# Output rows in two pieces of six products, read by ScalarE and summed by GpSimd, in a two-branch attention kernel

## The chip, the cores and the metric

The kernel runs on one core of a Trainium2 chip. The metric is the device time of one execution in microseconds (us). A core has a matrix engine (TensorE, PE in the profile; its weight loads are PEld), a vector engine (VectorE, DVE), a scalar engine (ScalarE, ACT), a general engine (GpSimd, POOL) and a queue that issues DMAs (SyncE, SP). Each engine works through its own list of instructions in order, and they wait for each other by semaphores. TensorE writes its results to PSUM, eight banks of 128 x 512 float32; the other tiles lie in SBUF.

## The reference, cut to what matters

The input x is 2048 x 512. Two attention branches with 32 heads of 16 columns share it, and a gate mixes them.

```
g = sigmoid(sum(x * gate_w))                      # one number a row
a = A(x): 4 segments of 512 rows; in each, causal softmax attention within the segment,
    plus a memory term phi(q) M / phi(q) z from the segments before; mixed by sigmoid(beta); @ wo
b = B(x): softmax attention over all 2048 rows; @ wo_b
out = g * a + (1 - g) * b
```

The part that the change touches works on the scaled attention outputs o of both branches: out = o_A @ wo + o_B @ wo_b, 128 rows at a time.

## The kernel before

**Units, slots, groups.** Queries are cut into four chunks of 512 rows, heads into eight quads. One (chunk, quad) is a unit: 32 of branch A (u = 0 to 31) and 32 of branch B (u = 32 to 63). The main loop has 32 slots; slot k computes unit 32 + k of B and then unit k of A. A slot has 37 groups n: 0 to 31 for the 16 key blocks of B (two heads each), 32 to 36 for the four key blocks of A. All instructions are written out in this order (`manual_schedule`), so the code's order is the order in each engine's list.

**What a group does.** `t_group` multiplies K with Q for two heads (L635) into two banks out of three (tb0, tb1, mb, the least lately used first; in slot 31 five, with two of the score banks), and ScalarE takes the exponential (L641) into one of two tile sets `raw`. Between the two products, in most groups, stands a score product for the next unit (`s_b`, L572, two matmuls into one of two buffers `sbk`), of which VectorE takes the row maxima (L574); in groups 32 to 36 these are scores of A (L550, L554, maxima L558, L560). Then `pvs` adds a V product (`pv`, L657): exponentials times V for four heads, into the one bank `pvb`. Key block `it` of B is multiplied in groups 2 it + 2 and 2 it + 3, 256 of the 512 queries in each. For A, GpSimd first sets the masked entries of the diagonal blocks to zero (L644). A's products are 0 in groups 34 and 35 by halves, 1 and 3 in group 36, and 2 in group 0 of the next slot.

**What follows a unit.** `fin_copy` copies `pvb` to a tile `pvs`: for B in group 33 and for A in group 0 of the next slot; `pvb` may be written again only then. By way of DRAM its sums come back as `rec`, VectorE takes the reciprocals (L681, groups 11 and 13), GpSimd scales them and, every second slot, normalises a whole output tile (`fin_norm`, L701, L706; it waits for the DMA that brings the factors `d`). `m_chain` (after group 21) and `m_rows` (group 24) turn the maxima into rows of the next unit's Q.

**Output rows.** From slot 8 on, at the end of every even slot, `out_split` splits 128 rows of o into a high and a low part (oh on ScalarE, L723; ol on GpSimd, L724). In group 1 of the next slot `out_mm` multiplies branch A's half of them (a = 0) with wo in twelve products (oh with wh, oh with wl, ol with wh, four each), and ScalarE copies the bank to `yo`; in group 1 of the slot after, branch B's half (a = 1), and VectorE adds the bank to `yo`, which is stored. The 24th, for which no slot is left, is in group 28 of slot 31. The last chunk's rows are done in a tail. The weights wo are loaded in group 19 and split by GpSimd (`split_wo`, L716, L717) in group 29 of slots 1 to 4.

Of the kernel before, what the change touches and what calls it, by code (L numbers as in the profile page):

```python
# [7 lines left out]
FT = mybir.dt.float32  # L8
# [4 lines left out]
AF = mybir.ActivationFunctionType  # L13
OP = mybir.AluOpType
# [7 lines left out]
DM = 512  # L22
C = 512
NC4 = SEQ // C
NT = SEQ // 128
# [8 lines left out]
S_LAST = 10  # L34
OMI = 14
SPILLS = 64


@with_exitstack
def gated_mix_kernel(ctx, tc, xt, wq, wk, wv, wo, beta, wqkv, wob, gate_w, out):  # L40
    nc = tc.nc
# [62 lines left out]
    PVB = PS.tile([128, C], FT, name="pvb")  # L104
# [11 lines left out]
    def misc():  # L116
        return bank(mode["misc"])
# [178 lines left out]
    TERMS = ((0, 0), (0, 1), (1, 0))  # L296
# [207 lines left out]
    def load_q(u):  # L504
        kd, qd, c = UN[u]
        load_qk(q_of(u), kd, 0, qd, c)
# [109 lines left out]
    AT = {}  # L616
# [30 lines left out]
    def pv(u, it, lo=0, hi=None):  # L647

        kd, qd, c = UN[u]
        g, q = divmod(qd, 2)  # L650
        q0 = 128 * it if kd == "A" else 0
        hi = hi or C - q0
        last = 2 if kd == "A" else NT - 1
        vt = VA[(u // 2) % 2] if kd == "A" else VB[g % 2]
        for h in range(4):
            pt = PT[u, it, h]
            nc.tensor.matmul(PVB[32 * h:32 * h + E + 1, q0 + lo:q0 + hi], vt[:, it, 4 * q + h, :], pt[:, lo:hi],  # L657
                             start=it == 0 and lo == 0, stop=it == last and q0 + hi == C, skip_group_check=True)

    def fin_copy(u):  # L660

        ps = W.tile([128, C], FT, name="pvs", bufs=1)
        if 8 <= u < 31:
            nc.vector.tensor_copy(ps, PVB)
        else:
            nc.scalar.activation(ps, PVB, AF.Copy)
        AT["pd", u] = D.tile([4, 32, C], FT, name=f"pd{u}")
        nc.sync.dma_start(AT["pd", u].rearrange("h r t -> (h r) t"), ps)

# [53 lines left out]
        nc.scalar.activation(AT["oh"], o_cols(c, t), AF.Copy)  # L723
        nc.gpsimd.tensor_tensor(AT["ol"], o_cols(c, t), AT["oh"], op=OP.subtract)  # L724

    def out_mm(c, t, a, inner=()):

        b = misc()
        for n, (oi, wi, g) in enumerate([(oi, wi, g) for oi, wi in TERMS for g in range(4)]):
            nc.tensor.matmul(b, (AT["oh"], AT["ol"])[oi][:, g, a], (AT["wh"], AT["wl"])[wi][:, g, a],  # L730
                             start=n == 0, stop=n == 11)
            if n == 5:
                for f in inner:
                    f()
        if a == 0:
            AT["yo"] = AT["L"].tile([128, DM], FT, name="yo")
            nc.scalar.activation(AT["yo"], b, AF.Copy)
        else:
            tt = 4 * c + t
            nc.vector.tensor_tensor(AT["yo"], b, AT["yo"], op=OP.add)  # L740
            nc.sync.dma_start(outr[tt * 128:(tt + 1) * 128, :], AT["yo"])

    def tail_ops(t):
# [31 lines left out]
    def todo(fn, *a):  # L775
        return lambda: fn(*a)
# [33 lines left out]
    for tt in range(NT):  # L810
        c, tl = divmod(tt, 4)
# [38 lines left out]
    for n in range(8):  # L850
        c, w = divmod(n, 2)
# [51 lines left out]
    for blk in range(16):  # L903
        g, c = divmod(blk, 4)
        pg, pc = divmod(blk - 1, 4)
        if blk == 4:
            mode["misc"] = TB + [MB, PVB]
        rate = len(ST_A + ST_B) / SPILLS if 4 <= blk < 14 else 0
        if blk == 14:
# [3 lines left out]
        n = blk + 1 + (c == 2)  # L913
# [106 lines left out]
    def pvs(k, n):  # L1020

        ua, ub = k, 32 + k
        if n == 0:
            if k:
                pv(ua - 1, 2)
                fin_copy(ua - 1)
        elif k == 31 and n < 2 * NT:
            if n % 2 and n > 1:
                pv(ub, n // 2 - 1)
        elif 2 <= n < 2 * NT + 2:  # L1030
            pv(ub, n // 2 - 1, n % 2 * 256, n % 2 * 256 + 256)
            if n == 2 * NT + 1:
                fin_copy(ub)
        elif n > 2 * NT + 1:
            m = n - 2 * NT - 2
            if m < 2:
                pv(ua, 0, 256 * m, 256 * m + 256)
            else:
                pv(ua, 1)
                pv(ua, 3)  # L1040

    def extras(k):

        pre, post = {}, {}
        if not k:
            for n in range(4):
                pre[2 * n] = [fill[n - 4]]
        post[2 * S_LAST + 4] = [todo(m_rows, k + 1)]
        for n, at in [(k - 9, 1)] + [(23, 2 * OMI)] * (k == 31):
            if n >= 0:  # L1050
                rows = (n // 8, n // 2 % 4, n % 2)
                pre[at] = [todo(out_mm, *rows)]
        return pre, post

    def beside(k, it):
# [49 lines left out]
    for k in range(32):  # L1105
        ua, ub = k, 32 + k
        banks = T3 + [b[:, 0] for b in SBK] * (k == 31)
        for n in range(NG):
            it = n // 2 if n < NG - 1 else NT + 2
            mid = plan.pop((k, n)) if n < 2 * NT and (k, n) in plan else []  # L1110
            t_group(*(ub, n) if n < 2 * NT else (ua, n - 2 * NT), banks, mid)
            for f in plan.get((k, n), []) + ex[k][0].get(n, []):
                f()
            pvs(k, n)
            for f in ex[k][1].get(n, []):
                f()
            if n % 2 == 0 and n < NG - 1:
                continue
            beside(k, it)
            if it == S_LAST:  # L1120
                m_chain(k + 1)
            if it == 4 and not k:
                late()
            if it == 4 and not k:
                load_q(ub + 2)
                for c in range(NC4):
                    load_kb(2, c)
            if it == NT and k < 29:
                load_q(ub + 3)
                load_kb(k + 3)  # L1130
            if it == 6 and k < 31:
                load_q(ua + 1)
                load_ka(ua + 1)
                if (ua + 1) % 2 == 0:
                    load_va(ua + 1)
            if it == 9:
                if k % 2 == 0 and k < 30:
                    load_vb(k // 2 + 1)
                if 1 <= k <= 4:
                    load_wo(k - 1)  # L1140
            if it == 14 and 1 <= k <= 4:
                split_wo(k - 1)
    pv(31, 2)
    fin_copy(31)
# [53 lines left out]
```

## Time and profile before

| | before |
|---|---|
| runs shown, us | 1809.66 median of 3 (1808.37 to 1809.92) |
| the profiled execution, us | 1811.22 |
| its span, us | 1809.5 |
| busy: PE, DVE, ACT, POOL, us | 1773.7, 1571.4, 1454.3, 323.1 |
| slot 0 starts at, slot 31 ends at, us | 325.2, 1783.0 |
| slots 5 to 8, without output rows, us each | 43.3 |
| slots 9 to 29, with them, us each | 45.4 to 45.7 |
| mean granted clock of TensorE | 0.997 |

Span is the time from the first to the last instruction. Times in rows of a timeline are from the span's start. A timeline's row gives the start, the length, the engine, the line of the code, the operation, output<-input, the shapes and how many instructions it joins; in brackets stands how long the engine had been idle ahead of it, and what ended that. The next instruction can start before the last one's end is recorded, so the cost of an instruction in a stream is read from start to start. A product in float32 stands in the trace as two matmuls, so a V product of four heads is x8.

### The profile page before, as it was taken

What the parts mean: (1) busy time and instruction counts of PE and PEld (TensorE: products, weight loads), DVE (VectorE), ACT (ScalarE), POOL (GpSimd) and SP (SyncE); (2) the same over time, 40 slices, a digit from 0 to 9 for tenths busy, and PEclk for the clock granted to TensorE, in tenths of its full rate; (3) what the DMA queues carried; (4) which work ended last, traced back from release to release, by engine and by line L of the source; (5) the groups of instructions that cost most, each with busy time, mean ns of one, the idle gap of its engine ahead of it and who ended that gap; (6) DMA issues with size and microseconds to landing.
All of it is one profiled execution on the core that took longest, in us unless ns stands there. A gap on an engine that the chain in (4) does not pass through costs nothing.

```text
span 1809.5 us, 43733 instructions
## 1 busy us (share of the span) xinstructions
PE 1773.7 (98%) x17517; PEld 636.5 (35%) x17517; DVE 1571.4 (87%) x1738; ACT 1454.3 (80%) x2738; POOL 323.1 (18%) x711
## 2 busy tenths in 40 slices
PE   8999999899999999999999999999999999999998
PEld 6554445222222222333333333333333333333325
DVE  7744786699999999999999999999999999999932
ACT  4454444599899999989898989898989898989894
POOL 4400000101222111112121212121212121212122
PEclk9999999999999999999999999999999999999999
DMA  5654534332323233232323232322323232322111
GB/s 198 153 148 141 158 105 114 77 80 78 94 79 92 68 87 81 63 93 63 91 65 87 69 85 71 83 74 66 88 77 80 71 79 68 89 68 85 47 36 62
DMA packets 162480, 158.89 MB, mean 88 GB/s; under 512 B 40140, under 2 KB 126620, under 8 KB 162276
## 3 DMA queue, kind: packets, MB, share of 16 engines
q1 hardware_dynamic: 158692, 149.29, 30.0%
q0 software_dynamic: 3296, 6.27, 1.8%
q8 instruction: 138, 2.26, 0.5%
q14 instruction: 66, 0.54, 0.1%
q10 hardware_dynamic: 288, 0.52, 0.1%
HBM read 103.38 MB, written 50.86 MB: 85 GB/s over the span
## 4 chain that ended last, share of the span: by engine, by line
PE 90%; DVE 4%; ACT 2%; DMA 2%; issue 1%; POOL 1%; SPq 0%; ACTq 0%; DVEq 0%; POOLq 0%
PE pvb L657 35%; PE tb L635 14%; PE sbk L572 11%; PE mb L635 7%; PE tb L332 3%; DVE mxb L574 3%; PE tb L730 3%; PE sbk L550 2%; PE mb L332 2%; PE tb L302 2%; PE sbk L302 2%; PE pvb L332 1%; PE mb L730 1%; ACT raw L641 1%; PE sbk L332 1%
## 5 line engine op out<-in xcount | busy, mean ns | idle before, releaser
L574 DVE TENSOR_REDUCE mxb<-sbk 128x2 f32<-128x1024 f32 x1024 | 1172.3, 1214 | 32.5 <-PE tb L635 19.9
L641 ACT ACTIVATE raw<-tb 128x512 f32<-128x512 f32 x1555 | 883.5, 599 | 73.0 <-PE tb L635 36.2
L657 PE MATMUL pvb<-raw,vb 128*17 128x256 f32 (+1 forms) x8072 | 643.4, 388 | 0.0
L572 PE MATMUL sbk<-kb,qb 64*128 64x512 f16 x2048 | 567.0, 378 | 4.5 <-DVE mxb L574 4.3
L641 ACT ACTIVATE raw<-mb 128x512 f32<-128x512 f32 x782 | 468.6, 599 | 39.7 <-PE mb L635 25.5
L635 PE MATMUL tb<-qb,kb 64*128 64x512 f16 x1342 | 467.5, 381 | 4.6 <-ACT raw L641 3.5
L635 PEld LDWEIGHTS <-kb 64*128 64x128 f16 x2048 | 136.9, 93 | 416.3 <-issue 411.5
L657 PEld LDWEIGHTS pvb<-raw,vb 128*17 128x17 f32 x8072 | 136.7, 95 | 406.2 <-issue 400.1
L635 PE MATMUL mb<-qb,kb 64*128 64x512 f16 x679 | 258.5, 381 | 0.0
L644 POOL TENSOR_SCALAR_AFFINE_SELECT raw<-raw 128x256 f32<-128x256 f32 (+1 forms) x320 | 115.5, 364 | 281.6 <-ACT raw L641 274.0
L558 DVE TENSOR_REDUCE mx<-sbk 128x2 f32<-128x1024 f32 (+1 forms) x128 | 134.1, 1088 | 9.9 <-PE sbk L554 8.6
L572 PEld LDWEIGHTS <-qb 64*128 64x128 f16 x2048 | 130.6, 93 | 27.5 <-issue 15.3
L657 PE MATMUL pvb<-raw,va 128*17 128x256 f32 (+2 forms) x1280 | 104.7, 383 | 5.7 <-POOL raw L644 2.2
L689 POOL TENSOR_TENSOR rec<-rec,grow 128x16 f32<-128x16 f32 x30 | 6.7, 222 | 444.9 <-DVE rec L681 444.9
L560 DVE TENSOR_REDUCE mx<-sbk 128x4 f32<-128x512 f32 x64 | 60.8, 950 | 12.4 <-PE sbk L554 12.4
L550 PE MATMUL sbk<-ka,qa 64*128 64x512 f16 (+3 forms) x512 | 70.7, 296 | 0.0
L701 POOL TENSOR_TENSOR o<-o,d 128x512 f32<-128x512 f32 x31 | 39.5, 1275 | 167.4 <-DMA d<-rd 155.0
L635 PE MATMUL tb<-qa,ka 64*128 64x512 f16 (+3 forms) x339 | 61.8, 302 | 0.0
L347 DVE SCALAR_TENSOR_TENSOR phi<-phe,phi 128x512 f32<-128x512 f32 x24 | 16.6, 693 | 51.6 <-ACT phe L346 51.6
L332 PEld LDWEIGHTS <-ws 128*128 128x128 f16 x384 | 37.5, 99 | 44.8 <-issue 5.2
L554 PE MATMUL sbk<-cmask,crows 64*128 64x64 bf16 x1024 | 52.7, 189 | 0.0
L554 PEld LDWEIGHTS <-crows 64*128 64x128 bf16 x1024 | 46.4, 94 | 14.0
(334 smaller groups left out, 1450.2 us busy)
## 6 DMA issues: line engine op xcount, KB each, us to landing
vb<-vdB SPq DMA_DIRECT2D x16, 1088.0 KB
pd<-pvs SPq DMA_DIRECT2D x64, 256.0 KB
kb<-dB SPq DMA_DIRECT2D x60, 256.0 KB
dB<-st SPq DMA_DIRECT2D x64, 128.0 KB
dA<-st SPq DMA_DIRECT2D x64, 128.0 KB
o<-pd SPq DMA_DIRECT2D x64, 128.0 KB
d<-rd SPq DMA_DIRECT2D x63, 128.0 KB
kb<-dB SPq DMA_DIRECT2D x60, 128.0 KB
```

The source lines that it names most:

```text
L302: nc.tensor.matmul(b, x[:, n % 4, tl * 128:(tl + 1) * 128], (WVA if kd == "A" else WV)[wi][:, n % 4, :], start=n == 0, stop=n == 11)
L332: nc.tensor.matmul(b, WS[ws][w][wi][:, k, :], (XH, XL)[xi][c][:, k, :], start=n == 0, stop=n == 11)
L550: nc.tensor.matmul(b[:, j, c0:c0 + n], q_of(u)[r, p, i * 128:(i + 1) * 128], k_of(u, p)[r, :n], start=True, stop=False)
L554: nc.tensor.matmul(b[:, j, c0 + n - 128 + w.start:c0 + n - 128 + w.stop], crows[r, n2 - 1], cmask[r, n2 - 1, w], start=False, stop=n2 == 2)
L558: nc.vector.tensor_reduce(m[:, :, p, i], b[:, :, :n], axis=AX.X, op=OP.max)
L572: nc.tensor.matmul(b[:, j], q_of(u)[r, p, i * 128:(i + 1) * 128], k_of(u, p)[r, kc * C:(kc + 1) * C], start=True, stop=True)
L574: nc.vector.tensor_reduce(MXB[u][:, :, p, i, kc], b, axis=AX.X, op=OP.max)
L635: nc.tensor.matmul(bs[j][:, c0:c0 + w], k_of(u, h // 2)[r, 128 * it:128 * it + 128], q_of(u)[r, h // 2, q0:], start=True, stop=True)
L641: nc.scalar.activation(pt, bs[j], AF.Exp, scale=AT["esc", kd, qd // 2])
L644: nc.gpsimd.affine_select(out=m, in_=m, pattern=[[1, 128]] if n < 2 else [[0, 2], [1, 128]], compare_op=OP.is_ge, fill=0.0, base=0, channe ...
L657: nc.tensor.matmul(PVB[32 * h:32 * h + E + 1, q0 + lo:q0 + hi], vt[:, it, 4 * q + h, :], pt[:, lo:hi], start=it == 0 and lo == 0, stop=it ...
L730: nc.tensor.matmul(b, (AT["oh"], AT["ol"])[oi][:, g, a], (AT["wh"], AT["wl"])[wi][:, g, a], start=n == 0, stop=n == 11)
```

## The change

- `out_mm` does six of the twelve products of an output row half (`PIECES`), and is called twice a slot, in groups 1 and 12 (`OUT_AT`); in slot 31 the second row's two pieces both stand in group 28. The first piece of a row is copied to `yo` by ScalarE; each of the other three is copied by ScalarE to a tile `yp` (one buffer) and added to `yo` by GpSimd. VectorE no longer takes part.
- Key block 5 of B is multiplied whole (`WHOLE`), 512 queries in group 13; group 12 has no V product.
- A's V product 3 goes from group 36 to group 0 of the next slot, behind product 2 (but in slot 31 stays).
- `fin_copy` is on ScalarE always; it was on VectorE for A's units 8 to 30.
- `split_wo` is written in group 25 instead of 29, ahead of the normalisation of group 27.

```diff
+OUT_AT = (1, 12)
+PIECES = ((0, 6), (6, 12))
+WHOLE = (5,)
 def pv(u, it, lo=0, hi=None):
-        last = 2 if kd == "A" else NT - 1
+        last = (3 if u < 31 else 2) if kd == "A" else NT - 1
 def fin_copy(u):
-        if 8 <= u < 31:
-            nc.vector.tensor_copy(ps, PVB)
-        else:
-            nc.scalar.activation(ps, PVB, AF.Copy)
+        nc.scalar.activation(ps, PVB, AF.Copy)
-    def out_mm(c, t, a, inner=()):
+    def out_mm(c, t, a, x):
+        lo, hi = PIECES[x]
         b = misc()
-        for n, (oi, wi, g) in enumerate([(oi, wi, g) for oi, wi in TERMS for g in range(4)]):
+        for n, (oi, wi, g) in enumerate([(oi, wi, g) for oi, wi in TERMS for g in range(4)][lo:hi]):
             nc.tensor.matmul(b, (AT["oh"], AT["ol"])[oi][:, g, a], (AT["wh"], AT["wl"])[wi][:, g, a],
-                             start=n == 0, stop=n == 11)
...
+                             start=n == 0, stop=n == hi - lo - 1)
-        if a == 0:
+        if (a, x) == (0, 0):
             AT["yo"] = AT["L"].tile([128, DM], FT, name="yo")
             nc.scalar.activation(AT["yo"], b, AF.Copy)
-        else:
+            return
+        y = AT["L"].tile([128, DM], FT, name="yp")
+        nc.scalar.activation(y, b, AF.Copy)
+        nc.gpsimd.tensor_tensor(AT["yo"], AT["yo"], y, op=OP.add)
+        if (a, x) == (1, len(PIECES) - 1):
             tt = 4 * c + t
-            nc.vector.tensor_tensor(AT["yo"], b, AT["yo"], op=OP.add)
             nc.sync.dma_start(outr[tt * 128:(tt + 1) * 128, :], AT["yo"])
 def pvs(k, n):
                 pv(ua - 1, 2)
+                pv(ua - 1, 3)
                 fin_copy(ua - 1)
-        elif k == 31 and n < 2 * NT:
-            if n % 2 and n > 1:
-                pv(ub, n // 2 - 1)
-        elif 2 <= n < 2 * NT + 2:
-            pv(ub, n // 2 - 1, n % 2 * 256, n % 2 * 256 + 256)
+        elif n < 2 * NT + 2:
+            it, h = n // 2 - 1, n % 2
+            if k == 31 and n < 2 * NT or it in WHOLE:
+                if h and it >= 0:
+                    pv(ub, it)
+            elif it >= 0:
+                pv(ub, it, 256 * h, 256 * h + 256)
...
                 pv(ua, 1)
-                pv(ua, 3)
+                if k == 31:
+                    pv(ua, 3)
 def extras(k):
-        for n, at in [(k - 9, 1)] + [(23, 2 * OMI)] * (k == 31):
-            if n >= 0:
-                rows = (n // 8, n // 2 % 4, n % 2)
-                pre[at] = [todo(out_mm, *rows)]
+        for n, ats in [(k - 9, OUT_AT)] + [(23, (2 * OMI,) * len(PIECES))] * (k == 31):
+            for x, at in enumerate(ats if n >= 0 else ()):
+                pre.setdefault(at, []).append(todo(out_mm, n // 8, n // 2 % 4, n % 2, x))
 main loop
-            if it == 14 and 1 <= k <= 4:
+            if it == 12 and 1 <= k <= 4:
                 split_wo(k - 1)
```

In the rows that follow, qb and kb are Q and K of B, va and vb the values of A and B, ident and the buffers' numbers don't matter, and a line number of the changed kernel is three higher from `pv` on.

TensorE before, from group 36 of slot 15 to the output row in group 1 of slot 16 (weight loads and score products left out):

```order
L657 MATMUL pvb<-raw_86,va_77 17x384 x4
L657 MATMUL pvb<-raw_86,va_77 17x128 x4
...
L635 MATMUL tb_134<-qb_68,kb_90 128x512
L657 MATMUL pvb<-raw_86,va_77 17x256 x4
...
L730 MATMUL tb_134<-wh,oh 128x512 x4
L730 MATMUL tb_134<-wl,oh 128x512 x4
L730 MATMUL tb_134<-wh,ol 128x512 x4
```

TensorE after, the same stretch:

```order
L660 MATMUL pvb<-raw_86,va_77 17x384 x4
...
L638 MATMUL mb<-qb_68,kb_90 128x512
L660 MATMUL pvb<-raw_86,va_77 17x256 x4
L660 MATMUL pvb<-raw_86,va_77 17x128 x4
...
L731 MATMUL mb<-wh,oh 128x512 x4
L731 MATMUL mb<-wl,oh 128x512 x2
```

The V product of 128 columns (A's block 3) now stands behind product 2 in group 0, and the output row ends after six products.

TensorE after, groups 12 and 13 of the same slot:

```order
L638 MATMUL tb_135<-qb_68,kb_90 128x512
L731 MATMUL tb_134<-wl,oh 128x512 x2
L731 MATMUL tb_134<-wh,ol 128x512 x4
...
L638 MATMUL tb_135<-qb_68,kb_90 128x512
L660 MATMUL pvb<-raw_86,vb_75 17x512 x4
```

Before, each of the two groups had a V product of 17x256; now group 12 has the other six output products and group 13 the whole block.

GpSimd before, from group 21 to 36 of slot 2:

```order
L595 TENSOR_TENSOR m_4223<-mx,mhi 128x32
L701 TENSOR_TENSOR o_2997<-o_2997,d_3001 128x512
L716 CAST wh<-o_2998 128x512
L717 TENSOR_TENSOR wl<-o_2998,wh 128x512
...
L644 AFFINE_SELECT raw_86<-raw_86 128x128 x4
```

GpSimd after, the same stretch:

```order
L598 TENSOR_TENSOR m_4211<-mx,mhi 128x32
L716 CAST wh<-o_2998 128x512
L717 TENSOR_TENSOR wl<-o_2998,wh 128x512
...
L701 TENSOR_TENSOR o_2997<-o_2997,d_3001 128x512
L647 AFFINE_SELECT raw_86<-raw_86 128x128 x4
```

The four instructions of the split stand ahead of the normalisation now (L701), no longer between it and the masks.

GpSimd after, slot 31 from group 12 on:

```order
L739 TENSOR_TENSOR yo<-yo,yp 128x512
L684 TENSOR_SCALAR rec<-rec,nq 128x16
L685 TENSOR_TENSOR rec<-rec,grow 128x16
L1082 TENSOR_TENSOR o_2998<-o_2998,d_3001 64x512
L739 TENSOR_TENSOR yo<-yo,yp 128x512 x2
L647 AFFINE_SELECT raw_86<-raw_86 128x128 x4
```

The two sums of the pieces in group 28 stand behind the product with the factors d (L1082, before L1078).

More of the change, by code (lines that the diff above doesn't have):

```diff
@@ L724, in out_split @@
         nc.gpsimd.tensor_tensor(AT["ol"], o_cols(c, t), AT["oh"], op=OP.subtract)
-    def out_mm(c, t, a, inner=()):
+    def out_mm(c, t, a, x):
+        lo, hi = PIECES[x]
         b = misc()
-        for n, (oi, wi, g) in enumerate([(oi, wi, g) for oi, wi in TERMS for g in range(4)]):
+        for n, (oi, wi, g) in enumerate([(oi, wi, g) for oi, wi in TERMS for g in range(4)][lo:hi]):
             nc.tensor.matmul(b, (AT["oh"], AT["ol"])[oi][:, g, a], (AT["wh"], AT["wl"])[wi][:, g, a],
-                             start=n == 0, stop=n == 11)
-            if n == 5:
-                for f in inner:
-                    f()
-        if a == 0:
+                             start=n == 0, stop=n == hi - lo - 1)
+        if (a, x) == (0, 0):
             AT["yo"] = AT["L"].tile([128, DM], FT, name="yo")
             nc.scalar.activation(AT["yo"], b, AF.Copy)
-        else:
+            return
[3 more added lines that the diff above has]
+        if (a, x) == (1, len(PIECES) - 1):
             tt = 4 * c + t
-            nc.vector.tensor_tensor(AT["yo"], b, AT["yo"], op=OP.add)
             nc.sync.dma_start(outr[tt * 128:(tt + 1) * 128, :], AT["yo"])
@@ L1025, in pvs @@
                 pv(ua - 1, 2)
+                pv(ua - 1, 3)
                 fin_copy(ua - 1)
-        elif k == 31 and n < 2 * NT:
-            if n % 2 and n > 1:
-                pv(ub, n // 2 - 1)
-        elif 2 <= n < 2 * NT + 2:
-            pv(ub, n // 2 - 1, n % 2 * 256, n % 2 * 256 + 256)
+        elif n < 2 * NT + 2:
[5 more added lines that the diff above has]
+                pv(ub, it, 256 * h, 256 * h + 256)
             if n == 2 * NT + 1:
                 fin_copy(ub)
-        elif n > 2 * NT + 1:
+        else:
             m = n - 2 * NT - 2
```

## The prediction

> **What bounds the kernel now.** I read the page's first part, then a table of windows, then the timelines of TensorE, VectorE, ScalarE and GpSimd in single slots, and the chain of waits last.
>
> ```profile
> PE 1773.7 (98%) x17517; PEld 636.5 (35%) x17517; DVE 1571.4 (87%) x1738; ACT 1454.3 (80%) x2738; POOL 323.1 (18%) x711
> 739.21:1694.12 954.91, 953.05 (x10586) 303.22 (x10586) 913.76 (x893) 859.27 (x1618) 175.81 (x399) 1.00 0.29 77
> ```
>
> The second row (columns: window, length, busy time of PE, PEld, DVE, ACT, POOL, granted clock) holds slots 9 to 29: 954.91 / 21 = 45.47 us a slot. TensorE is never idle there, but busy is a modelled end, so the row doesn't tell whether TensorE or VectorE (96%) sets the pace. The cadence does: windows of slot 16, cut at the starts of groups 2, 11, 24 and 25, with the score products counted (two to a group).
>
> ```profile
> 1061.95:1071.80 9.85, 5.38 (x18) 0.96 (x18) 1.00 0.17 54
> 1071.80:1086.70 14.90, 6.93 (x26) 2.03 (x26) 1.00 0.46 127
> 1086.70:1088.16 1.46, 0.42 (x2) 0.18 (x2) 1.00 0.22 53
> 1088.16:1095.88 7.72, 4.11 (x14) 0.82 (x14) 1.00 0.07 19
> ```
>
> Nine groups take 9.85 us, 1.094 each: TensorE's own pace. The thirteen groups 11 to 23 take 14.90, which is 0.67 more than 13 x 1.094. VectorE's timeline of the same slot says why.
>
> ```profile
> 1059.16 0.68 DVE L664 COPY pvs<-pvb 128x512 f32<-128x512 f32 x1
> ...
> 1062.06 0.69 DVE L740 TENSOR_TENSOR yo<-tb,yo 128x512 f32<-128x512 f32 x1 [1.08 <-PE tb L730]
> 1062.67 11.40 DVE L574 TENSOR_REDUCE mxb<-sbk 128x2 f32<-128x1024 f32 x10
> 1073.98 0.24 DVE L681 RECIPROCAL rec<-rec 128x16 f32<-128x16 f32 x1
> ...
> 1076.50 9.08 DVE L574 TENSOR_REDUCE mxb<-sbk 128x2 f32<-128x1024 f32 x8
> 1085.49 0.21 DVE L583 TENSOR_REDUCE mx<-mxb 128x16 f32<-128x64 f32 x1
> ```
>
> Ten maxima take 11.31 us from the first start to the reciprocal's, 1.131 each, against TensorE's 1.094. VectorE falls back 0.037 us a group, and 0.16 at each of two reciprocals (start to start, groups 11 and 13), 0.13 at L583 (group 21). There are two score buffers; when it is some 0.4 us behind, TensorE waits, from group 11 on. Yet in group 1 VectorE had nothing to do (1.08 us of idle ahead of the output sum, more in odd slots): it can't catch up later with that. TensorE then was in one output row of twelve products:
>
> ```profile
> 1058.48 0.39 PE L635 MATMUL mb<-qb,kb 64*128 64x512 f16 x1
> ...
> 1059.01 1.20 PE L730 MATMUL tb<-wh,oh 128*128 128x512 f32 x4
> 1060.05 1.07 PE L730 MATMUL tb<-wl,oh 128*128 128x512 f32 x4
> 1060.96 1.07 PE L730 MATMUL tb<-wh,ol 128*128 128x512 f32 x4
> 1061.96 0.39 PE L635 MATMUL mb<-qb,kb 64*128 64x512 f16 x1
> ```
>
> Group 1 takes 3.48 us: 0.53 until the row, 2.95 for it (1.04 for the first four, 0.91 for the next, 1.00 with the tail of 0.32).
>
> **The change, part by part (slots 9 to 29).** *Two pieces.* Six products take 1.04 + 0.23 + 0.32 = 1.59, so group 1 falls from 3.48 to 2.12. Group 12 has no V product now: 0.53 + 1.59 = 2.12 instead of 1.09. *Block 5 whole* in group 13, from the chain of waits (half a block at the slots' pace, a whole one in slot 31):
>
> ```profile
> 1700.43 0.56 PE pvb L657 x8
> ...
> 1772.55 0.98 PE pvb L657 x8
> ```
>
> 0.54 + 0.98 = 1.52 instead of 1.09. Sum over groups 1, 12, 13: 5.76 against 5.67, a loss of 0.1 us. What it buys: VectorE needs 1.13 in group 12, where 2.12 go by, and 1.29 with its reciprocal in group 13, where 1.52 go by. It enters group 12 some 0.33 + 0.16 behind and leaves group 13 level. From there 0.037 x 8 + 0.13 brings it to 0.43 at group 22, the edge of what two buffers bear: I leave 0.05 of waiting. Gone are 0.67 (groups 11 to 23), 0.13 (group 24, the third window, begins with the wait that L583 leaves) and 0.06 (7.72 less 7 x 1.094). Net 0.67 + 0.13 + 0.06 - 0.05 - 0.10 = 0.71 a slot, 14.9 us over 21 slots; 0.35 in slot 30, which has score products only until group 19.
>
> *VectorE's work* falls by the copy (0.6 start to start) and every second slot by the sum (0.6). That lies where it idled, so I count nothing; the new bound is TensorE, and without the pieces' second idle of VectorE this cover would be needed.
>
> *ScalarE* gets 0.49 more for the copy and one to two output pieces more (0.49 each, start to start). Its queue holds the exponentials behind them, and TensorE waits for those through three banks. The row of an odd slot where it reads the output already:
>
> ```profile
> 1016.60 0.60 ACT L737 ACTIVATE yo<-tb 128x512 f32<-128x512 f32 x1 [2.01 <-PE tb L730]
> ```
>
> It had idled 2.01 us: a row of products feeds it nothing. A piece of 1.59 leaves it about 1.1 less the copy's 0.49. The bank it reads is wanted again in the group after next, 1.09 us later, and a reading takes 0.60. Bounds: nothing, or 0.49 a slot. I take nothing, nearest to this row, since the cadence behind it was 1.09.
>
> *GpSimd* gets 36 sums of about 1.28 (row 468.15 below is such a sum); it is 18% busy. The output's store waits for the last sum, 2.12 + 0.6 + 1.28 = 4 us after group 12's start, and behind it in SyncE's queue stand the broadcast of the reciprocals and the loads of the next A unit. GpSimd's product that needs the broadcast stands at group 19, seven groups on: I count nothing.
>
> *V product 3 of A* moves over the slot's edge: 128 columns, by the chain's rows (0.98 - 0.56) / 2 = 0.21 us, leave group 36 and join group 0. In slots 9 to 29 that is nothing. In slots 1 to 8, without output rows, TensorE stands for ScalarE in group 2 (slot 7, TensorE and then ScalarE):
>
> ```profile
> 653.16 0.63 PE L657 MATMUL pvb<-raw,va 128*17 128x256 f32 x8
> ...
> 655.47 0.80 PE L657 MATMUL pvb<-raw,vb 128*17 128x256 f32 x8
> ```
>
> ```profile
> 654.02 0.60 ACT L666 ACTIVATE pvs<-pvb 128x512 f32<-128x512 f32 x1
> ```
>
> The copy started 0.23 after the V product's 0.63: there is room for 0.21. The scores come 0.21 earlier, and the wait hides the product: 0.2 x 8 = 1.6 us. Their block 5 brings nothing, since groups 12 to 23 go at VectorE's pace.
>
> *split_wo earlier.* Slot 2, GpSimd, then TensorE:
>
> ```profile
> 468.15 1.28 POOL L701 TENSOR_TENSOR o<-o,d 128x512 f32<-128x512 f32 x1 [7.96 <-DMA d<-rd]
> 469.36 0.63 POOL L716 CAST wh<-o 128x512 fp32r<-128x512 f32 x1
> ...
> 473.19 1.76 POOL L644 TENSOR_SCALAR_AFFINE_SELECT raw<-raw 128x128 f32<-128x128 f32 x6
> ```
>
> ```profile
> 473.54 1.34 PE L657 MATMUL pvb<-raw,va 128*17 128x256 f32 x8 [1.09 <-POOL raw L644]
> 462.00:464.00 2.00, 2.00 (x26) 0.49 (x24) 2.00 (x3) 1.99 (x4) 0.00 (x0) 1.00 0.04 12
> ```
>
> The split (3.83 us) stands behind a normalisation that waits 7.96 us for its factors, and the masks behind the split; TensorE loses 1.09 and 1.34 - 0.63. Moved ahead, the split runs in that wait: the window says that the DMA engines were done with its 512 KB by 462. 1.8 us in slot 2, the same in slot 4, 3.6 together; at worst nothing.
>
> *Slot 31* has no maxima, and ScalarE sets its pace. Its idle times, and GpSimd:
>
> ```profile
> 1743.53 0.60 ACT L737 ACTIVATE yo<-mb 128x512 f32<-128x512 f32 x1 [1.80 <-PE mb L730]
> 1772.65 1.08 ACT L641 ACTIVATE raw<-sbk 128x512 f32<-128x512 f32 x2 [2.04 <-PE sbk L635]
> ```
>
> ```profile
> 1771.87 1.27 POOL L1078 TENSOR_TENSOR o<-o,d 64x512 f32<-64x512 f32 x1 [22.88 <-DMA d<-rd]
> ```
>
> The first idle shrinks by 1.36 less V product 3: a gain of 1.2. The piece in group 12 costs its reading and a gap behind 1.59 us without food, 0.8. In group 28 two pieces follow each other; both land in the one buffer yp, so the second reading waits for GpSimd's first sum, and that for L1078: 1771.87 + 1.27 + 1.28 + 0.5 gives 1775.0 for the next exponential, not 1772.65. Later gaps give some back: a loss of 1.9. Slot 31 loses 1.5 (bounds: a gain of 1, a loss of 3).
>
> Sum: 14.9 + 0.35 + 1.6 + 3.6 - 1.5 = 19 us. The profiled execution took 1811.22 us (1809.5 and 1.7 around it), 1.6 over the median of 1809.66; from the median this is 1790.7. I say 1791.
>
> **Rivals.** *ScalarE late.* For it: in slot 7 the copy on ScalarE is part of TensorE's wait. Against it: the 2.01 us idle of the odd slots. At 0.49 a slot it costs 10.3 us: 1801. It would end the gain at 0.9 a slot.
>
> *VectorE stays the bound*: the second idle comes too early, and the waits of groups 13 to 24 come back in full. For it: the forecast has VectorE at 0.43 of about 0.4 by group 22. Against it: it is level nine groups before. 0.8 x 21 = 17 us: 1808, no change.
>
> *GpSimd holds VectorE up*, the one that ends slower: while a sum runs, maxima stand still. In odd slots a sum falls on groups 13 and 14 and puts VectorE 1.28 back: 0.88 of waiting, and 0.2 to 0.3 more as it then paces the rest, 1.1; in even slots a second one in group 2, 2.4. 11 x 1.1 + 10 x 2.4 = 36 us: 1827. It decides from 0.6 us of VectorE's time a sum (19 us over 31 sums). Against it: eight maxima of slot 16 (row 1076.50) ran 1.12 apart across this sum:
>
> ```profile
> 1079.74 1.28 POOL L701 TENSOR_TENSOR o<-o,d 128x512 f32<-128x512 f32 x1 [2.42 <-DMA d<-rd]
> ```
>
> The Trainium skill speaks for this rival: Perfetto Trace Analysis, section Optimizing Scalar/DVE Operations, has the two share an SBUF read port, "so offloading operations between those two might not help". Its page SBUF — State Buffer, section SBUF: two separate sides, narrows that to VectorE instructions with two SBUF inputs or a two-port mode. By the broad sentence the time is 1827, by the narrow one nothing changes, as a maximum reads PSUM; the trace's 1.12 sides with the narrow one.
>
> **How the numbers follow.** The forecast has 0.73, with a range of its own of 1785 to 1797: split_wo may give nothing (+3.6), slot 31 lie 1.5 to 2.5 off either way, the pieces cost 0.1 a slot more or less (2 us). ScalarE late 0.13, VectorE bound 0.06, GpSimd 0.04, an unseen loss 0.03, an unseen zero 0.01. About 0.2% (3.6 us) is what a measurement tells from no change: faster 0.86, same 0.07, slower 0.07. 1785 to 1803 takes in the second case and holds 0.8.
>
> **What would show it.** Slots 9 to 29 near 44.75 us; groups 11 and 14 to 23 at 1.094; VectorE idle in groups 1, 12 and 13; TensorE's wait of 1.09 in slots 2 and 4 gone; slots 5 to 8 at 0.2 less; slot 31 longer, with ScalarE waiting for GpSimd in group 28. Wrong would be: groups 2, 3, 13 or 14 over their sums with waits for ScalarE's readings, or maxima above 1.22 beside GpSimd's sums.

## The result, and the profile after

The changed kernel takes 1794.93 us (median of 4 runs, 1794.82 to 1795.03), the kernel before 1809.38 on the same chip (4 runs, 1808.37 to 1809.92): 14.45 us less, ratio 0.9916, 95% interval 0.9903 to 0.9928. The forecast was 1791 within 1785 to 1803.

The profiled execution of the changed kernel took 1794.91 us, with a span of 1793.19. First the busy line of its page, and the window of slots 9 to 29 (length, then busy time of PE, PEld, DVE, ACT, POOL, granted clock).

```profile
PE 1756.5 (98%) x17269; PEld 613.7 (34%) x17269; DVE 1559.4 (87%) x1703; ACT 1476.2 (82%) x2797; POOL 369.5 (21%) x747
734.86:1677.04 942.18, 940.31 (x10419) 284.89 (x10418) 902.32 (x862) 878.67 (x1670) 215.12 (x430) 1.00 0.29 78
```

942.18 / 21 = 44.87 us a slot, where it was 45.47. By the start of each slot's first score product (slot 31, which has none, by its first product of K and Q), the two spans split like this (us):

| part | before | after | change | forecast |
|---|---|---|---|---|
| up to slot 1 | 389.01 | 388.87 | -0.14 | 0 |
| slots 1 to 8 | 350.20 | 345.99 | -4.21 | -5.2 |
| slots 9 to 29 | 954.91 | 942.18 | -12.73 | -14.9 |
| slot 30 | 44.84 | 44.40 | -0.44 | -0.35 |
| slot 31 to the end | 70.54 | 71.75 | +1.21 | +1.5 |
| span | 1809.50 | 1793.19 | -16.31 | -19 |

The profiled execution of before lay 1.84 us over its median of 1809.38, that of after at its median. So 16.3 us of span are 14.45 us of medians.

Slot 16 again, in windows cut at the starts of groups 1, 2, 11, 24, 25 and 32, with the score products counted (PE, PEld, clock, DMA share, GB/s).

```profile
1050.12:1052.24 2.12, 0.60 (x2) 0.11 (x2) 1.00 0.92 199
1052.24:1062.10 9.86, 5.39 (x19) 0.97 (x19) 1.00 0.20 57
1062.10:1077.79 15.69, 7.77 (x26) 1.40 (x27) 1.00 0.40 116
1077.79:1079.22 1.43, 0.46 (x2) 0.18 (x3) 1.00 1.13 285
1079.22:1086.93 7.71, 4.11 (x14) 0.81 (x14) 1.00 0.06 19
```

Group 1 takes 2.12 instead of 3.48. Groups 11 to 23 take 15.69: eleven at 1.094 are 12.03, and groups 12 and 13, by the starts of their score products, took 2.13 and 1.52. That is all, so the 0.67 of waiting is gone. Group 24 took 1.46 and takes 1.43; groups 25 to 31 are unchanged. There the forecast expected 0.19 less and 0.05 of new waiting.

VectorE in the same slot (start, us, idle before it in brackets):

```profile
1052.88 11.41 DVE L577 TENSOR_REDUCE mxb<-sbk 128x2 f32<-128x1024 f32 x10 [0.90 <-PE tb L638]
1064.21 0.24 DVE L681 RECIPROCAL rec<-rec 128x16 f32<-128x16 f32 x1
1064.37 1.16 DVE L577 TENSOR_REDUCE mxb<-sbk 128x2 f32<-128x1024 f32 x1
1065.96 1.23 DVE L577 TENSOR_REDUCE mxb<-sbk 128x2 f32<-128x1024 f32 x1 [0.44 <-PE tb L638]
1067.11 0.24 DVE L681 RECIPROCAL rec<-rec 128x16 f32<-128x16 f32 x1
1067.48 9.14 DVE L577 TENSOR_REDUCE mxb<-sbk 128x2 f32<-128x1024 f32 x8
```

It now idles twice, 0.90 after group 1 and 0.44 after group 12, and enters the second half of the slot level with TensorE. (Line numbers are three higher than before up to `pv`, so L577 was L574 and L586 was L583; from `fin_copy` to `split_wo`, L681, L701 and L716 for example, they are the same.)

Slot 2, GpSimd: the split (L716, L717) stands ahead of the normalisation and runs while that waits for its factors; the masks (L647) come as soon as ScalarE has written the blocks.

```profile
461.91 0.61 POOL L716 CAST wh<-o 128x512 fp32r<-128x512 f32 x1 [1.95 <-DMA o<-in_A_wo_dram]
...
467.71 1.27 POOL L701 TENSOR_TENSOR o<-o,d 128x512 f32<-128x512 f32 x1 [1.93 <-DMA d<-rd]
470.27 0.29 POOL L647 TENSOR_SCALAR_AFFINE_SELECT raw<-raw 128x128 f32<-128x128 f32 x1 [1.29 <-ACT raw L644]
```

TensorE's first V product of A, which waited 1.09 us for the masks before, follows without idle time:

```profile
472.58 0.63 PE L660 MATMUL pvb<-raw,va 128*17 128x256 f32 x8
```

Slots 2 and 4 fell from 44.98 and 44.96 to 43.40 and 43.22 us. The other end of the balance is slot 31, ScalarE and then GpSimd:

```profile
1753.34 0.60 ACT L738 ACTIVATE yp<-tb 128x512 f32<-128x512 f32 x1 [0.34 <-PE tb L731]
1756.26 0.60 ACT L738 ACTIVATE yp<-mb 128x512 f32<-128x512 f32 x1 [2.32 <-PE tb L638]
```

```profile
1753.72 1.28 POOL L1082 TENSOR_TENSOR o<-o,d 64x512 f32<-64x512 f32 x1 [14.61 <-DMA d<-rd]
1754.96 1.26 POOL L739 TENSOR_TENSOR yo<-yo,yp 128x512 f32<-128x512 f32 x1
1756.93 1.27 POOL L739 TENSOR_TENSOR yo<-yo,yp 128x512 f32<-128x512 f32 x1 [0.71 <-ACT yp L738]
```

The second reading starts 0.04 after the first sum ends (1754.96 + 1.26 = 1756.22), which began when L1082 was done. The bracket names TensorE; the order of the rows says GpSimd.

### The profile page after: what moved, and what is told of

The parts are those of the page before. It is cut to its first block, busy times and chain, and to the rows that moved or that the text cites. A ratio compares the mean times of both kernels' runs of the same rounds, so it can differ in the third digit from the quotient of the medians.

```text
span 1793.2 us, 43247 instructions
## 1 busy us (share of the span) xinstructions
PE 1756.5 (98%) x17269; PEld 613.7 (34%) x17269; DVE 1559.4 (87%) x1703; ACT 1476.2 (82%) x2797; POOL 369.5 (21%) x747
## 4 chain that ended last, share of the span: by engine, by line
PE 88%; DVE 8%; ACT 2%; DMA 1%; issue 1%; SPq 0%; ACTq 0%; DVEq 0%; POOLq 0%
PE pvb L660 34%; PE tb L638 13%; PE sbk L575 11%; PE mb L638 7%; DVE mxb L577 7%; PE tb L335 3%; PE tb L731 3%; PE sbk L553 2%; PE mb L335 2%; PE tb L305 2%; PE sbk L305 2%; PE pvb L335 2%; PE mb L731 1%; PE sbk L335 1%; PE sbk L557 1%; PE pvb L305 1%
## 5 line engine op out<-in xcount | busy, mean ns | idle before, releaser
L577 DVE TENSOR_REDUCE mxb<-sbk 128x2 f32<-128x1024 f32 x1024 | 1176.5, 1213 | 41.9 <-PE tb L638 19.0
L660 PE MATMUL pvb<-raw,vb 128*17 128x256 f32 (+1 forms) x7824 | 637.0, 395 | 0.0
L575 PE MATMUL sbk<-kb,qb 64*128 64x512 f16 x2048 | 587.7, 380 | 6.3 <-DVE mxb L577 6.1
L638 PE MATMUL tb<-qb,kb 64*128 64x512 f16 x1339 | 461.5, 381 | 4.9 <-ACT raw L644 3.8
L638 PEld LDWEIGHTS <-kb 64*128 64x128 f16 x2048 | 122.8, 94 | 433.5 <-issue 414.8
L660 PEld LDWEIGHTS pvb<-raw,vb 128*17 128x17 f32 x7824 | 132.5, 95 | 397.1 <-issue 391.0
L647 POOL TENSOR_SCALAR_AFFINE_SELECT raw<-raw 128x256 f32<-128x256 f32 (+1 forms) x320 | 115.7, 362 | 284.9 <-ACT raw L644 277.0
L575 PEld LDWEIGHTS <-qb 64*128 64x128 f16 x2048 | 115.8, 94 | 26.6 <-issue 21.0
L701 POOL TENSOR_TENSOR o<-o,d 128x512 f32<-128x512 f32 x31 | 39.5, 1274 | 170.3 <-DMA d<-rd 167.7
L739 POOL TENSOR_TENSOR yo<-yo,yp 128x512 f32<-128x512 f32 x36 | 45.9, 1274 | 80.8 <-ACT yp L738 76.9
```

The costliest lines, as they stand in the source:

```text
L575: nc.tensor.matmul(b[:, j], q_of(u)[r, p, i * 128:(i + 1) * 128], k_of(u, p)[r, kc * C:(kc + 1) * C], start=True, stop=True)
L577: nc.vector.tensor_reduce(MXB[u][:, :, p, i, kc], b, axis=AX.X, op=OP.max)
L638: nc.tensor.matmul(bs[j][:, c0:c0 + w], k_of(u, h // 2)[r, 128 * it:128 * it + 128], q_of(u)[r, h // 2, q0:], start=True, stop=True)
L647: nc.gpsimd.affine_select(out=m, in_=m, pattern=[[1, 128]] if n < 2 else [[0, 2], [1, 128]], compare_op=OP.is_ge, fill=0.0, base=0, channe ...
```

## The experiments

Theory: what counts is where VectorE's idle time lies in the slot, not how much work it has. Rival A: the gain is VectorE's lighter work (A's copy and the output sums left it). Rival B: GpSimd's sums hold VectorE up. Rival C: slots 9 to 29 are now at ScalarE's limit. Each edit is against the changed kernel; every run stands against the kernel before on its own chip.

**The output row in one piece, VectorE still relieved.**

```
-OUT_AT = (1, 12)
-PIECES = ((0, 6), (6, 12))
-WHOLE = (5,)
+OUT_AT = (1,)
+PIECES = ((0, 12),)
+WHOLE = ()
```

> The changed kernel with the output row again in one piece of twelve products in group 1 (no whole block 5); A's copy stays on ScalarE, the row is read by ScalarE and summed by GpSimd. If the spread of the idle time is what counts: the 0.67 us of waits in groups 11 to 23 return, TensorE's 0.10 for two pieces is saved, 0.57 x 21 = 12 us, and slot 31 gets back some 1.5 us (one reading less): about 1805 us. If VectorE's lighter work made the gain: no waits return, 1795 less 2 and less 1.5, about 1791.

1805.45 us (10 runs), ratio 0.9975 (0.9966 to 0.9985).

```profile
734.66:1687.80 953.14, 951.28 (x10585) 301.73 (x10584) 896.94 (x862) 871.66 (x1649) 187.87 (x409) 1.00 0.29 77
1112.41:1127.25 14.84, 7.01 (x26) 1.96 (x27) 1.00 0.22 59
```

The first row is slots 9 to 29, 45.39 each; the second groups 11 to 23 of slot 17, with 14.84 - 13 x 1.094 = 0.62 of waits back. VectorE has the 862 operations of the changed kernel, 31 fewer than before, and the time is nearly that of before. Rival A falls.

**The second piece early.** The same products, readings and sums; the place differs, and with it the block that is taken whole.

```
-OUT_AT = (1, 12)
-WHOLE = (5,)
+OUT_AT = (1, 4)
+WHOLE = (1,)
```

> The changed kernel with its second piece in group 4 in place of group 12 (and block 1 whole in place of block 5): the same products, readings and sums, only the place differs. If what counts is that VectorE gets a second idle time late in the slot, most of it is lost: VectorE is level after group 5 and then falls back 0.037 us a group and 0.16 at each reciprocal, so the waits of groups 11 to 23 come back less 3 x 0.037, 0.56 us in each of slots 9 to 29: 12 us, about 1807 us. If the gain came from the work that VectorE no longer has (copy and output sums), it stays near 1795.

1805.99 us (10 runs), ratio 0.9981 (0.9971 to 0.9990); slots 9 to 29 take 952.28, 10.10 more than in the changed kernel (12 were expected). VectorE in slot 16:

```profile
1056.60 3.49 DVE L577 TENSOR_REDUCE mxb<-sbk 128x2 f32<-128x1024 f32 x3 [0.90 <-PE tb L638]
1060.91 1.23 DVE L577 TENSOR_REDUCE mxb<-sbk 128x2 f32<-128x1024 f32 x1 [0.82 <-PE mb L638]
1062.43 6.88 DVE L577 TENSOR_REDUCE mxb<-sbk 128x2 f32<-128x1024 f32 x6 [0.29 <-PE tb L638]
```

It idles 0.90 + 0.82 + 0.29 = 2.01 us by group 5, more than the 0.90 + 0.44 of the changed kernel, and 0.48 a slot of waiting returns from group 14 on (groups 14 to 23 at 1.13 where they were 1.09, group 16 at 1.24 behind a reciprocal). Idle time early in the slot can't be saved up: this is the cleanest run for the theory.

**VectorE copies and sums again, pieces where they are.**

```
+        if 8 <= u < 31:
+            nc.vector.tensor_copy(ps, PVB)
+        else:
+            nc.scalar.activation(ps, PVB, AF.Copy)
...
-        nc.scalar.activation(y, b, AF.Copy)
-        nc.gpsimd.tensor_tensor(AT["yo"], AT["yo"], y, op=OP.add)
+        nc.vector.tensor_tensor(AT["yo"], b, AT["yo"], op=OP.add)
```

> The changed kernel with its two pieces where they are, but VectorE copies A's result again in slots 8 to 30 and adds every piece but a row's first to yo itself (no yp, no sums on GpSimd). If the place of the pieces is what counts, VectorE's second idle time covers this: 12 and 13 take 3.65 us, VectorE then needs 0.49 behind + 1.73 + 1.29 = 3.5. In odd slots group 1 holds copy, sum and maximum, 2.3 against 2.12, a loss of at most 0.2 in every second slot; slot 31 gains about 2 since no reading waits for GpSimd: 1793 to 1796 us. If VectorE's lighter work made the gain, 0.6 to 1.2 us a slot come back as waits: 1805 or more.

1795.61 us (4 runs), ratio 0.9919 (0.9904 to 0.9934), the changed kernel's to within its interval.

```profile
736.29:1679.46 943.17, 941.31 (x10417) 285.76 (x10416) 929.28 (x914) 856.04 (x1618) 175.59 (x399) 1.00 0.29 78
```

```profile
1052.21 0.68 DVE L667 COPY pvs<-pvb 128x512 f32<-128x512 f32 x1
...
1053.97 0.69 DVE L740 TENSOR_TENSOR yo<-mb,yo 128x512 f32<-128x512 f32 x1
...
1067.13 0.68 DVE L740 TENSOR_TENSOR yo<-tb,yo 128x512 f32<-128x512 f32 x1
```

VectorE is busy for 929.28 of 943.17 us, 98.5%, and slots 9 to 29 are only 1.0 longer (0.05 a slot). The copy and the two sums of this slot (the rows are slot 16's) lie where VectorE idled. Of the two halves of the change, the place of the products made the gain and the move to ScalarE and GpSimd nearly none: the 1.0 us that it gains in these slots it loses again in slot 31, which takes 70.28 with VectorE's sums and 71.75 without. (This trace also reaches slot 1 1.4 us later, at 390.29, though the edit doesn't touch that part; the equal medians alone don't show the parts.) ScalarE works 22.6 us less in slots 9 to 29 (856.04 for 878.67), and they don't get shorter: rival C falls too, for pieces of six products.

**A second GpSimd pass behind each sum.**

```
         nc.gpsimd.tensor_tensor(AT["yo"], AT["yo"], y, op=OP.add)
+        nc.gpsimd.tensor_tensor(y, AT["yo"], y, op=OP.subtract)
```

> The changed kernel with a second GpSimd pass of the same shape behind each sum of pieces (yp is written over with yo less yp, which nothing reads), 36 passes of about 1.26 us more. If GpSimd's passes don't hold VectorE up, slots 9 to 30 are unchanged; slot 31 gets about 1 us longer, since ScalarE's reading in group 28 waits for yp: 1796. If they do hold it up, by 0.6 to 1.28 us each, 18 to 40 us more: 1813 or more.

1796.74 us (5 runs), ratio 0.9926 (0.9913 to 0.9940). Slots 9 to 29 and VectorE's ten maxima of slot 16:

```profile
734.86:1677.10 942.24, 940.36 (x10418) 284.93 (x10418) 902.30 (x862) 878.66 (x1670) 253.52 (x461) 1.00 0.29 78
1052.91 11.40 DVE L577 TENSOR_REDUCE mxb<-sbk 128x2 f32<-128x1024 f32 x10 [0.90 <-PE tb L638]
```

GpSimd works 38.4 us more there, and 942.24 against 942.18 is no difference: rival B falls. The Trainium skill (Perfetto Trace Analysis, section Optimizing Scalar/DVE Operations) has the broad sentence that offloading between these two engines might not help since they share a read port; taken at its word, each pass would have cost VectorE time, and none did. The narrower statement of its page SBUF — State Buffer, section SBUF: two separate sides, agrees. What the kernel is longer by, 1.8 us by the medians, is slot 31's (73.81 for 71.75), where the reading in group 28 stands behind the extra pass, and now the bracket names it:

```profile
1757.81 0.60 ACT L738 ACTIVATE yp<-mb 128x512 f32<-128x512 f32 x1 [3.68 <-POOL yp L740]
```

**Three pieces.**

```
-OUT_AT = (1, 12)
-PIECES = ((0, 6), (6, 12))
-WHOLE = (5,)
+OUT_AT = (1, 10, 20)
+PIECES = ((0, 4), (4, 8), (8, 12))
+WHOLE = (4, 9)
...
-        y = AT["L"].tile([128, DM], FT, name="yp")
+        y = AT["L"].tile([128, DM], FT, name="yp", bufs=2)
```

> The changed kernel with the output row in three pieces of four products in groups 1, 10 and 20 (blocks 4 and 9 whole) and two buffers yp. If the wait left in group 24 (about 0.1 us) and those of groups 25 to 31 (0.06) are VectorE's lag since group 13, a third idle time at groups 20 and 21 takes them away: 0.16 less some 0.08 for one more piece on TensorE, 0.1 x 21 = 2 us, and slot 31 gains about 1 by the second yp: 1791 to 1793 us. If these waits have another cause (the chain of the row maxima behind group 21), slots 9 to 29 are 0.08 longer each: 1795 to 1797. If ScalarE has no room for a third reading, 0.49 x 21 = 10 us: 1805.

1797.23 us (5 runs), ratio 0.9929 (0.9916 to 0.9943): 4 us over what was expected, and at the end of the range for waits with another cause. Slot 31 gained nothing (71.70): with three pieces in group 28 the last reading waits for one of the two buffers again (2.19 us, behind GpSimd's sum). Group 24 and groups 25 to 31, in slot 22:

```profile
1349.53:1350.83 1.30, 0.60 (x2) 0.11 (x3) 1.00 1.04 314
1350.83:1358.52 7.69, 4.19 (x14) 0.75 (x14) 1.00 0.07 22
```

The time alone doesn't tell the causes apart; these rows do: the wait of group 24 is VectorE's lag and goes with it (1.30 for 1.43), while groups 25 to 31 hardly change (7.69 for 7.71). But the third piece costs even slots what it saves (44.85, as in the changed kernel), and odd ones take 44.95: group 2 takes 1.20 us. In odd slots ScalarE has split o just before (L723), which even slots don't have, and from there to group 2 it has no gap (from start to start 0.95 behind L723, then 0.47 to 0.49; slot 23):

```profile
1365.04 1.06 ACT L723 ACTIVATE oh<-o 128x1024 fp32r<-128x1024 f32 x1
...
1366.94 0.62 ACT L666 ACTIVATE pvs<-pvb 128x512 f32<-128x512 f32 x1
1367.42 0.63 ACT L644 ACTIVATE raw<-tb 128x512 f32<-128x512 f32 x1
...
1368.37 0.66 ACT L735 ACTIVATE yo<-tb 128x512 f32<-128x512 f32 x1
1368.86 0.67 ACT L644 ACTIVATE raw<-tb 128x512 f32<-128x512 f32 x1
```

Slot 22, an even one, has the same two extra readings (the copy and a piece), ScalarE idles 0.55 ahead of them, and nothing is late. By these rows a first piece of four products is too short for the copy and a reading right behind that split: rival C is true of pieces of four, in the odd slots. (No run moves the split alone.) And slots 1 to 8, which have whole blocks 4 and 9 without any piece, take 43.33 instead of 43.13, 1.3 us in all.

**Block 5 in halves.**

```
-WHOLE = (5,)
+WHOLE = ()
```

> The changed kernel with V product 5 again in two halves, one in each of groups 12 and 13 (the second piece stays in group 12). Its two halves of 0.54 us stand against 0.98 for the whole: TensorE does 0.12 more a slot, 21 x 0.12 = 2.5 us. Group 12 then takes 2.68 and group 13 1.09, so the reciprocal of group 13 falls into a group without spare time and VectorE leaves group 13 up to 0.2 behind; the waits of groups 22 to 24 grow by at most that, 4 us more. Between 1797.4 and 1801.6 us; I take 1799. If block 5 whole is nothing (the halves hide in VectorE's waits), 1795.

1801.13 us (5 runs), ratio 0.9951 (0.9937 to 0.9964), at the far end of what was expected. Slots 9 to 29, and groups 11 to 23 of slot 15:

```profile
734.85:1683.03 948.18, 946.31 (x10586) 292.57 (x10586) 899.30 (x862) 882.52 (x1670) 214.65 (x430) 1.00 0.30 77
1018.90:1034.83 15.93, 7.59 (x26) 1.61 (x27) 1.00 0.20 55
```

0.29 a slot more: groups 12 and 13 take 2.69 and 1.10 instead of 2.13 and 1.52, and groups 21 to 24 wait 0.03 to 0.04 each. Block 5 whole is worth 6.0 us here, since it gives group 13 the time that VectorE's second reciprocal needs.

**V product 3 of A back in group 36.**

```
-        last = (3 if u < 31 else 2) if kd == "A" else NT - 1
+        last = 2 if kd == "A" else NT - 1
...
-                pv(ua - 1, 3)
...
-                if k == 31:
-                    pv(ua, 3)
+                pv(ua, 3)
```

> The changed kernel with A's V product 3 back in group 36 (slots 0 to 30). By the prediction's step it was worth 0.2 us in each of slots 1 to 8: 1.6 us more, 1796.5. By the two traces it was worth 0.12 there, 1.0 us: 1795.9. In slots 9 to 29 nothing: TensorE does the same work on the other side of the edge. If the score products' earlier start mattered there too, 0.2 x 21 = 4 us more: 1800.

1796.09 us (5 runs), ratio 0.9921 (0.9907 to 0.9934). Slots 1 to 8 are 0.88 longer (slots 5 to 8 take 43.25 for 43.13), slots 9 to 29 take 942.38: nothing. The step is worth 0.12 a slot, not 0.2. Slot 7 of the changed kernel shows why, TensorE and then ScalarE:

```profile
649.14 0.85 PE L660 MATMUL pvb<-raw,va 128*17 128x256 f32 x16
```

```profile
649.52 0.59 ACT L644 ACTIVATE raw<-tb 128x512 f32<-128x512 f32 x1
650.10 0.60 ACT L666 ACTIVATE pvs<-pvb 128x512 f32<-128x512 f32 x1
```

The products end at 649.99 and the copy starts 0.11 later, 0.58 after the exponential, where before it followed after 0.48. Half of the 0.21 comes back as ScalarE's wait.

**The split behind block 14 again.**

```
-            if it == 12 and 1 <= k <= 4:
+            if it == 14 and 1 <= k <= 4:
```

> The changed kernel with the split of wo and wob back behind block 14 in slots 1 to 4. If GpSimd's order was the cause of TensorE's wait in slots 2 and 4, the waits come back there alone: 1.6 and 1.7 us, 1798.2 us. If those slots became shorter by something else (V product 3 moved), less than 0.5 us: 1795.

1798.04 us (5 runs), ratio 0.9931 (0.9917 to 0.9944). Only slots 2 and 4 change, to 44.35 and 44.54: 2.3 us, where 3.3 were expected. GpSimd and TensorE of slot 2:

```profile
467.22 1.27 POOL L701 TENSOR_TENSOR o<-o,d 128x512 f32<-128x512 f32 x1 [7.47 <-DMA d<-rd]
...
472.25 1.75 POOL L647 TENSOR_SCALAR_AFFINE_SELECT raw<-raw 128x128 f32<-128x128 f32 x6
```

```profile
472.60 1.34 PE L660 MATMUL pvb<-raw,va 128*17 128x256 f32 x8 [0.32 <-POOL raw L647]
```

The chain is the same one (factors, normalisation, split, masks, V product), but TensorE waits 0.32 and not 1.09 ahead of the V product, since the normalisation starts some 0.4 us earlier in the slot than before. GpSimd's order is the cause; its price hangs on when the factors land. The median is 3.1 over that of the changed kernel; 0.8 of that is slot 31 and the end (72.51 for 71.75), which in four kernels with the same code there ran from 71.75 to 72.70 us.

**Two buffers yp.**

```
-        y = AT["L"].tile([128, DM], FT, name="yp")
+        y = AT["L"].tile([128, DM], FT, name="yp", bufs=2)
```

> The changed kernel with two buffers for yp in place of one. The trace of the changed kernel names TensorE for ScalarE's second reading in group 28 of slot 31 (2.32 us of idle), but its order and GpSimd's rows say that it waits for the first sum, which stands behind a late normalisation. If so, ScalarE no longer waits there: 1.9 us less in slot 31, about 1793.0 us, slots 9 to 30 unchanged. If TensorE is the cause as the row says, nothing changes: 1795.

1793.73 us (4 runs), ratio 0.9910 (0.9895 to 0.9925). ScalarE in slot 31:

```profile
1753.39 0.60 ACT L738 ACTIVATE yp<-tb 128x512 f32<-128x512 f32 x1 [0.28 <-PE tb L731]
1754.84 0.60 ACT L738 ACTIVATE yp<-mb 128x512 f32<-128x512 f32 x1 [0.85 <-PE mb L731]
```

The idle time falls from 2.32 to 0.85, which is the second piece's own products; slot 31 takes 70.32 instead of 71.75, and slots 9 to 29 stay within 0.5. So the wait was for the buffer, and the bracket that named TensorE was wrong. The medians of this run and the changed kernel's come from different chips, and their intervals overlap: the gain of 1.4 (1.9 were expected) is read from the trace. It is clear of the spread of this slot: 70.32 here and 70.41 in the last run below with two buffers, 71.75 to 72.70 in the four with one.

**The reduction of the row maxima off VectorE** (L586, by six small GpSimd operations in place of it).

```
+            for n in (2, 1):
+                t = W.tile([128, 16, n], FT, name=f"mx{n}")
+                o = t if n > 1 else mx[:, 1].rearrange("q h i -> q (h i)").rearrange("q (a c) -> q a c", c=1)
+                nc.gpsimd.tensor_tensor(t, v[:, :, :n], v[:, :, n:], op=OP.subtract)
+                nc.gpsimd.tensor_scalar(t, t, 0.0, None, op0=OP.max)
+                nc.gpsimd.tensor_tensor(o, t, v[:, :, n:], op=OP.add)
+                v = t
```

> The changed kernel with L586, the reduction of the row maxima over the key quarters on VectorE (0.20 us, about 0.14 from start to start), left out of VectorE's queue in slots 1 to 30: GpSimd forms the same maxima by six small operations on 128x32 and 128x16 (b + max(a - b, 0), twice). If TensorE's wait left in group 24 (0.13 to 0.15 us ahead of its score product) is VectorE's lag with L586 on top, it shrinks to about 0.03: 0.1 x 21 = 2.2 us, and in slots 1 to 8, which go at VectorE's pace, 0.14 x 8 = 1.1 us: about 1791.7 us. If the wait has another cause (the products of the row maxima in group 24), slots 9 to 29 stay at 44.87 and the time is 1794 to 1795. If GpSimd's ten small operations are late for those products, group 24 grows: 1797 or more.

1792.72 us (4 runs), ratio 0.9904 (0.9889 to 0.9919). Slots 9 to 29 take 940.06, 2.1 less than in the changed kernel (2.2 expected), and slots 1 to 8 are 0.9 less. Group 24 of slot 17, and GpSimd's last row of the chain:

```profile
1121.15:1122.47 1.32, 0.57 (x2) 0.13 (x3) 1.00 0.04 12
```

```profile
1120.59 0.24 POOL L607 TENSOR_TENSOR m<-mx,mhi 128x32 f32<-128x32 f32 x1
```

Group 24 falls from 1.44 (slot 17 of the changed kernel) to 1.32, and GpSimd's ten operations end at 1120.83, before group 24 begins. The wait left there was VectorE's lag with L586 on top. The median lies 1.0 over the 1791.7 expected: slot 31 takes 72.70 in this trace, at the far end of its spread, though its code is unchanged.

**The last two together.**

> Two steps together: the reduction of the row maxima formed by GpSimd (six small operations in place of L586) and two buffers yp. The second alone took 1.4 us from slot 31. If both are independent, as they lie in different slots: 1791.7 less 1.4, about 1790.3 us, faster than both kernels. If the first gives nothing, 1793.7.

1790.84 us (4 runs), ratio 0.9894 (0.9879 to 0.9909), 0.5 from what was expected. The trace adds up: slots 9 to 29 940.27, slot 31 70.41. It is the fastest kernel of the study, 19 us under before on its chip and by its median 4 us under the changed kernel, though against the latter the intervals of the two ratios overlap.

## Why the prediction was right, and where its sizes were off

- **The two idle times** (the main term): right. Groups 1, 12 and 13 took 2.12, 2.13 and 1.52 as worked out, and the 0.67 of waits in groups 11 to 23 went. The piece moved early, and the row in one piece, bring 0.48 and 0.62 of them back.
- **Groups 24 to 31**: wrong, 0.11 a slot, 2.3 us, the whole miss of slots 9 to 29. The step that failed is "brings it to 0.43 at group 22, the edge of what two buffers bear: I leave 0.05 of waiting. Gone are ... 0.13 ... and 0.06". The lag itself was right: in slot 17 VectorE starts its maximum 0.64 us after the group's start in group 14 (level) and 1.07 in group 22, 0.43 behind. The edge was wrong; the prediction took it as some 0.4. VectorE from group 22 on, and TensorE at the start of group 24 (the first product of K and Q, then the score product):

```profile
1121.51 6.87 DVE L577 TENSOR_REDUCE mxb<-sbk 128x2 f32<-128x1024 f32 x6
```

```profile
1122.62 0.39 PE L638 MATMUL mb<-qb,kb 64*128 64x512 f16 x1
1122.77 0.45 PE L575 MATMUL sbk<-kb,qb 64*128 64x512 f16 x2
```

  With two buffers, the score product of group 24 writes where the maximum of group 22 reads. That maximum, the first of the six, ends at 1121.51 + 1.21 = 1122.72, and the product starts 0.05 later, 0.15 behind its group's start. The same 0.05 lies between the two in groups 11 to 24 of slot 16 before, wherever a score product is late. A maximum takes 1.214 us (the mean before) and the gap is 0.053 to a third place, so it may start up to 2 x 1.094 - 1.214 - 0.053 = 0.92 behind its group's start before TensorE waits: the edge is 0.28 behind level, and 0.43 less 0.28 is the 0.15. Before, the score product of group 24 was 0.18 late, so 0.03 is gone and not 0.13. Groups 25 to 31 didn't gain: group 24 takes TensorE 0.21 longer by its products of the row maxima (1.30 with three pieces, where nothing waits, less 1.094), and VectorE then starts 0.85 behind group 25 in the changed kernel as it started 0.84 behind it before.
- **VectorE's lighter work at nothing**: right; with the work back on VectorE, slots 9 to 29 are 1.0 us longer in all.
- **ScalarE at nothing**: right for pieces of six: groups 2, 3 and 14 of slot 16 take TensorE's own 1.09, and with less on ScalarE the slots don't get shorter. Pieces of four show the limit.
- **GpSimd's sums at nothing**: right; doubled, they cost slots 9 to 29 nothing.
- **V product 3**: right in kind, 0.12 a slot and not 0.2, 1.0 us and not 1.6. The words "there is room for 0.21" took the whole 0.23 between TensorE's product and the copy as spare; 0.11 of it goes by from the last product to ScalarE's start in any case, and 0.12 was left.
- **split_wo**: 3.6 forecast. Slots 2 and 4 fell by 1.58 and 1.74, less 0.13 each for V product 3: 3.1. That block 5 whole brings nothing in slots 1 to 8 was right of slots 5 to 8 (43.13 with it whole and in halves). Slots 2 and 4 take 43.13 too with block 5 in halves, so taking it whole costs them 0.27 and 0.09 of the 0.5 that is missing here; why isn't settled.
- **Slot 31**: 1.2 lost where 1.5 were forecast, by the mechanism named: the second yp takes it away. That the sizes agree to 0.3 is in part luck, since the same code took from 71.75 to 72.70 there, and the 1.9 of the wait for yp was 1.4.
- **The start**: some 1.6 of the 3.9 us between 1791 and 1794.93 are no term of the sum. I took the sum from a trace that was 1.6 over the median then shown and carried it to that median whole; the changed kernel's execution had no such surplus. Which slots held it isn't settled: there is one trace of the kernel before.

## What to carry to other kernels

Where two engines run at nearly one pace (here 1.131 against 1.094 us), the follower's idle time counts only where it comes: put the leader's extra work where the follower is about to run out of buffers, and split it if one place can't do. How far the follower may fall behind follows from the buffers: with two, the time of two groups, less one of its operations and the time from its end to the next write. Work that limit out from the rows before a lag is called harmless. A reading that moves to a third engine needs a second buffer as soon as two follow each other, or that engine's queue becomes a wait.

## What the runs showed of the hardware that was not expected

The idle column misled. The page's group of score products, in before, in the changed kernel and with the row in one piece (busy and mean ns, then the idle time just before and its main releaser):

```profile
L572 PE MATMUL sbk<-kb,qb 64*128 64x512 f16 x2048 | 567.0, 378 | 4.5 <-DVE mxb L574 4.3
```

```profile
L575 PE MATMUL sbk<-kb,qb 64*128 64x512 f16 x2048 | 587.7, 380 | 6.3 <-DVE mxb L577 6.1
```

```profile
L575 PE MATMUL sbk<-kb,qb 64*128 64x512 f16 x2048 | 567.9, 378 | 4.5 <-DVE mxb L577 4.3
```

It shows more waiting for VectorE after the change (6.1 for 4.3), though by the starts of the groups some 14 us of it are gone (0.67 in each of 21 slots). The waits lie under the recorded ends of the products before; the starts are what to count. The Trainium skill (Perfetto Trace Analysis, section Tensor Engine Instruction (MATMUL, LD_WEIGHTS)) says that a matmul's reported end is estimated from the instruction's size and not observed; the rows fit that.
